# A linear-attention block on one core: two x tiles transposed on TensorE instead of three, the last head group padded to the full array, VectorE's part of each q tile placed apart in the order, and the last output tile cut finer

## The chip, the cores and the metric

The kernel runs on one core of one Trainium2 chip. Times are device microseconds of one execution; medians are over repeated runs. A profile shows one execution. Its span, from the first to the last instruction, is about 1.4 us shorter than the time of the same execution (100.7 against 102.13 us in the profiled run of before). In every profile here the granted TensorE clock is given as 1.000, so a kernel's runs are told apart by their times: a run more than 1.5% above the fastest one of the same kernel is called slow and left out of the ratios.

Three names recur. *Before* is the kernel before, *after* the changed one, and *the whole change* is after as well, where experiments are compared with it.

## The reference

```python
B, S, D = x.shape                 # 1, 2048, 640
H = 32; Dh = D // H               # 32 heads of 20
qkv = (x @ wqkv).reshape(B, S, 3, H, Dh).transpose(2, 0, 3, 1, 4)
q, k, v = qkv[0], qkv[1], qkv[2]
phi = lambda t: jnp.where(t > 0, t + 1, jnp.exp(t)) + 1e-6
pq, pk = phi(q), phi(k)
kv = jnp.einsum("bhsd,bhse->bhde", pk, v)
z = jnp.einsum("bhsd->bhd", pk)
num = jnp.einsum("bhqd,bhde->bhqe", pq, kv)
den = jnp.einsum("bhqd,bhd->bhq", pq, z)[..., None] + 1e-6
return (num / den).transpose(0, 2, 1, 3).reshape(B, S, D) @ wo
```

All inputs and the output are bf16.

## The kernel before

The work on TensorE comes in stages:

- *K*: `x·wk` per tile of 128 rows; ScalarE and VectorE turn it into `pk`.
- *P*: `xᵀ·pk`, 640x640, accumulated over the 16 row tiles in two column halves. V itself is never formed: `wvᵀ·P` gives K·V.
- *q tiles*: `x·wq`, 20 pieces of 128 columns by 512 rows, put between the other matmuls.
- *K·V groups and folds*: six groups of six heads (120 columns; the last has two heads, 40 columns). Each is masked to its block diagonal on VectorE and multiplied by its rows of `wo` ("fold").
- *den*: the denominators, in two halves ("pairs"); their inverses are spread over the partitions by DMA and multiplied into `pq` ("normalize").
- *output*: `pq·folded wo`, 16 row tiles.

A scheduler class records every operation with the names it reads and writes, and derives the semaphore waits. **Every engine's instructions are emitted in the order of recording**, so where an operation is recorded decides what it queues behind: in before, VectorE starts the mask at 68.05 us, after the add recorded ahead of it (67.71 us, once the relu is there), though the last K·V matmul had started at 67.06 us. The parts that the change touches:

```python
GW, NG = 120, 6
gsz = [min(GW, D - GW * g) for g in range(NG)]       # 120 x5, 40
...
NPE = 3          # x tiles transposed on TensorE; the others by DMA transpose
XCH = [(0, 128), (128, 256), (256, 384),
       (384, 640), (640, 1024), (1024, 1536), (1536, 2048)]
...
# loads at the start, by queue: w01 is weight chunk 0 of wk, x12 is x tile 1
for eng, what in (("sp", "w01 w23 w34 x23"), ("act", "x12 w12 w45")):
...
def q_tile(sbk, c, b, two_act=False):
    ...                                    # five matmuls of 512 columns into bank b
    P.add("act", ... activation(t, bank(b), Exp) ...)
    if two_act:
        P.add("act", ... activation(r, bank(b), Relu) ...)
    P.add("dve", ... tensor_scalar(t, t, 1.0, 1e-6, min, add) ...)
    if two_act:
        P.add("dve", ... tensor_tensor(dst, t, r, add) ...)    # waits for the relu
        return
    P.add("dve", ... scalar_tensor_tensor(dst, bank(b), 0.0, t, max, add) ...)

def kv_group(h, b):                        # K.V of three groups
    for g in range(3 * h, 3 * h + 3):
        n = gsz[g]
        m = 128 if g < 5 else n            # the last group: a 128x40 array
        for d in range(NC_):
            e.matmul(bank(b, n, off=128 * (g % 3), parts=m), wv[...+ m], pt[...+ n], ...)

def w2_half(g, h, b):                      # half a fold
    n = gsz[g]                             # the last group: a 40x40 array
    e.matmul(bank(b, HALF, parts=n), kvt[0:n, GW * g:GW * g + n], wog[0:n, ...], ...)
...
# one letter per recorded step: p P step, q/Q q tile (Q: relu on ScalarE), z/s sums of pk for the
# denominators, k/K first and second K.V group with its mask, 0 to 5 folds, n normalize, i/I den,
# T output tile
for a in "qzzppzppzzpppqpQppqppppQppzQQkzQpp2zqpQppppsppppi0pqqpppp1npnpnQKnnQn35Qnn4qnqqQQnTT
          ITnTnnTTnnnnTnTTnnTTTTTT":
    step[a]()
```

(`...` marks the cuts.)

Of the kernel before, what the change touches and what calls it, by code (L numbers as in the profile page):

```python
# [7 lines left out]
ALU = mybir.AluOpType  # L8
# [9 lines left out]
class Plan:  # L18
# [6 lines left out]
    def __init__(self, nc, es):  # L25
        self.nc, self.es = nc, es
        self.sem = {e: es(nc.semaphore(f"s_{e}")) for e in self.ENGINES}
        self.count = {e: 0 for e in self.ENGINES}
        self.ops = {e: [] for e in self.ENGINES}
        self.known = {e: {} for e in self.ENGINES}  # L30
        self.writers, self.readers = {}, {}
        self.n_dma = 0
        self.sem_obj = {f"e:{e}": s for e, s in self.sem.items()}

    def add(self, eng, fn, reads=(), writes=(), dma=False, after=()):
        op = Op()
        op.eng, op.fn, op.dma = eng, fn, dma
        deps = list(after)
        for r in reads:
            w = self.writers.get(r)  # L40
            if w is None:
                raise KeyError(f"nothing wrote {r}")
            if not (w.eng == "pe" and eng == "pe"):
                deps.append(w)
        for r in writes:
            for d in [self.writers.get(r)] + self.readers.get(r, []):
                if d is not None and (d.dma or dma or d.eng != eng):
                    deps.append(d)
        known = self.known[eng]
        waits = {}  # L50
        for d in sorted(set(deps), key=lambda o: -o.val):
            if known.get(d.sem, 0) >= d.val:
                continue
            waits[d.sem] = max(waits.get(d.sem, 0), d.val)
            for s, v in d.clock.items():
                known[s] = max(known.get(s, 0), v)
            known[d.sem] = max(known.get(d.sem, 0), d.val)
        op.waits = list(waits.items())
        if dma:
            key = f"d:{self.n_dma}"  # L60
            self.sem_obj[key] = self.es(self.nc.semaphore(f"s_dma{self.n_dma}"))
            self.n_dma += 1
            op.sem, op.val, op.inc = key, 16, 16
        else:
            self.count[eng] += 1
            op.sem, op.val, op.inc = f"e:{eng}", self.count[eng], 1
        op.clock = dict(known)
        self.ops[eng].append(op)
        for r in reads:
            self.readers.setdefault(r, []).append(op)  # L70
        for r in writes:
            self.writers[r] = op
            self.readers[r] = []
        return op
# [8 lines left out]
def bass_standalone__linear_attn_block__prompt_kernel(nc, x, wqkv, wo, out):  # L83
    B, S, D = x.shape
    assert (B, S, D) == (1, 2048, 640)
    H, DH = 32, 20
    NC_ = D // 128
    NT = S // 128
# [7 lines left out]
    with contextlib.ExitStack() as ctx:  # L96
# [50 lines left out]
        def pool_const():  # L147
            P.add("pool", lambda e: e.memset(ident[:, :], 0.0), writes=["ident"])
            P.add("pool", lambda e: e.affine_select(
                out=ident[:, :], in_=ident[:, :], pattern=[[-1, 128]], base=0,  # L150
                channel_multiplier=1, compare_op=ALU.not_equal, fill=1.0),
                reads=["ident"], writes=["ident"])
            P.add("dve", lambda e: e.memset(eps[:, :], 1e-6), writes=["eps"])
            P.add("pool", lambda e: e.memset(wv[:, NC_ * D:], 0.0), writes=["wvpad"])
            P.add("pool", lambda e: e.memset(hm[:, :], 1.0), writes=["hm"])

            def band(t, pat, base, mult, name):

                v = t.rearrange("p (a b) -> p a b", b=pat[1][1])
                P.add("pool", lambda e: e.affine_select(  # L160
                    out=v, in_=v, pattern=pat, base=base, channel_multiplier=mult,
                    compare_op=ALU.is_ge, fill=0.0), reads=[name], writes=[name])


            band(hm[:, :], [[-4, 32], [0, 1]], 0, 1, "hm")
            band(hm[:, :], [[4, 32], [0, 1]], 3, -1, "hm")

            P.add("pool", lambda e: e.memset(bm[:, :], 1.0), writes=["bm"])
            for lo in (True, False):
                band(bm[:, :], [[-DH if lo else DH, NG], [0, DH]],  # L170
                     0 if lo else DH - 1, 1 if lo else -1, "bm")


        NPE = 3
        XCH = [(0, 128), (128, 256), (256, 384),
               (384, 640), (640, 1024), (1024, 1536), (1536, 2048)]

        def xch_of(row):
            return next(i for i, (a, b) in enumerate(XCH) if a <= row < b)
# [50 lines left out]
        def load_wk():  # L230
# [4 lines left out]
            for eng, lo in (("sp", 0), ("act", HALF)):  # L235
                P.add(eng, lambda e, lo=lo: e.dma_start(
                    xn[:, lo:lo + HALF], x[0, 0:128, lo:lo + HALF]),
                    writes=[("xn", 0, lo)], dma=True)
            for eng, what in (("sp", "w01 w23 w34 x23"), ("act", "x12 w12 w45")):
                for k in what.split():  # L240
                    a, b = int(k[1]), int(k[2])
                    if k[0] == "x":
# [9 lines left out]

        def load_rest():
            w_cols(wqn, 0, D, 0, "wqn", "sp")
            for a, b in ((3, 8), (8, 12), (12, 16)):
                load_xn(a, b, "sp")
            w_cols(wv, 0, D, 2 * D, "wv", "sp")
            P.add("sp", lambda e: e.dma_start(
# [60 lines left out]
                      reads=[("bank", d)], writes=[("pt", d, h)])  # L319

        nq = [0]

        def q_tile(sbk, c, b, two_act=False):
            i = nq[0] % 4
# [14 lines left out]
            if two_act:  # L339
                r = rq[i]  # L340
                P.add("act", lambda e: e.activation(r[:, :], bank(b), ACTF.Relu),  # L341
                      reads=[("bank", b), "table"], writes=[("rq", i)])
            P.add("dve", lambda e: e.tensor_scalar(  # L343
                t[:, :], t[:, :], 1.0, 1e-6, ALU.min, ALU.add),
                reads=[("eq", i)], writes=[("eq", i)])
            dst = pq[:, c * S + BK * sbk:c * S + BK * (sbk + 1)]
            if two_act:
                P.add("dve", lambda e: e.tensor_tensor(dst, t[:, :], rq[i][:, :], ALU.add),  # L348
                      reads=[("rq", i), ("eq", i)], writes=[("pq", sbk, c)])
                return  # L350
            P.add("dve", lambda e: e.scalar_tensor_tensor(  # L351
                pq[:, c * S + BK * sbk:c * S + BK * (sbk + 1)], bank(b), 0.0, t[:, :],
                ALU.max, ALU.add),
                reads=[("bank", b), ("eq", i)], writes=[("pq", sbk, c)])

        def z_add(dst, d_ap, a, b, ra, rb):
            P.add("dve", lambda e: e.tensor_tensor(d_ap, a, b, ALU.add),  # L357
# [48 lines left out]
        def kv_group(h, b):  # L406

            def mm(e):
                for g in range(3 * h, 3 * h + 3):
                    n = gsz[g]  # L410
                    m = 128 if g < 5 else n
                    for d in range(NC_):
                        r = e.matmul(  # L413
                            bank(b, n, off=128 * (g % 3), parts=m),
# [16 lines left out]
                    writes=[("kvt", g) for g in range(lo, lo + n)])  # L431

        def w2_half(g, h, b):
            n = gsz[g]
            P.add("pe", lambda e: e.matmul(  # L435
                bank(b, HALF, parts=n), kvt[0:n, GW * g:GW * g + n],
                wog[0:n, g * D + HALF * h:g * D + HALF * (h + 1)], start=True, stop=True),
                reads=[("kvt", g), "wog", "wog5"], writes=[("bank", b)])

        def w2_group(g, b):  # L440
# [71 lines left out]
        def out_dma(st, lo, hi, eng="sp"):  # L512
            j = st % 4
            P.add(eng, lambda e: e.dma_start(
                out[0, 128 * st:128 * st + 128, lo:hi], osb[j][:, lo:hi]),
                reads=[("osb", j, c) for c in range(lo // 160, hi // 160)],
                writes=[("out", st, lo)], dma=True)
            out_keys.append(("out", st, lo))

# [1 line left out]

        def out_evac(st, b, lo, hi, eng):
            j = st % 4
            keys = [("osb", j, c) for c in range(lo // 160, hi // 160)]
            if eng == "act":
                P.add("act", lambda e: e.copy(osb[j][:, lo:hi], bank(b, hi - lo)),  # L526
                      reads=[("bank", b)], writes=keys)
# [8 lines left out]
            out_evac(st, b + 1, HALF, D, "dve")  # L536
            out_dma(st, 0, D)

        def out_last(st, b):
            q = HALF // 2  # L540
            for n, (lo, hi, eng) in enumerate(((0, HALF, "act"), (HALF, HALF + q, "act"),
                                               (HALF + q, D, "dve"))):
                out_mm(st, b[n], lo, hi)
                out_evac(st, b[n], lo, hi, eng)
            out_dma(st, 0, HALF + q)
            out_dma(st, HALF + q, D, "act")


        pool_const()
        load_wk()  # L550
# [2 lines left out]
        warm(6)  # L553
        transpose_x(0, (6, 7), ("dve", "act"))
        warm(1)
        order = "t1 k00 k10 k01 k11 k02 k12 k03 k13 t2 k04 k14"
        for k in order.split():
            st = int(k[1])
            if k[0] == "t":
                transpose_x(st, *{1: ((4, 5), ("dve", "act")), 2: ((6, 7), ("dve", "act"))}[st])  # L560
            else:
                for h in range(2):
                    k_half(st, h, (int(k[2]),))
        for st in range(2):
            k_phi(st)
        for st in range(2, NT):
            for cs in ((0, 1), (2, 3, 4)) if st < 3 else (range(NC_),):
                for h in range(2):
                    k_half(st, h, cs)
            k_phi(st)  # L570
        zst = z_steps()
        qs = [(s, c) for s in range(NSB) for c in range(NC_)]
# [71 lines left out]
        def next_out():  # L644
            st = tiles.pop(0)
            out_tile(st, pair(st))
            if st == 1:
                small[:] = [1]

        step = {"p": lambda: steps.pop(0)(),  # L650
                "q": next_q, "Q": lambda: next_q(True), "z": lambda: zst.pop(0)(),
                "n": lambda: work(1), "s": lambda: z_finish(take()),
                "i": lambda: inverse(0), "I": lambda: inverse(1),
                "k": early_kv, "0": lambda: fold_wo(0), "1": lambda: fold_wo(1),
                "2": lambda: fold_wo(2), "K": late_kv, "3": lambda: late_w2(3),
                "4": lambda: late_w2(4), "5": lambda: late_w2(5), "T": next_out}
        for a in "qzzppzppzzpppqpQppqppppQppzQQkzQpp2zqpQppppsppppi0pqqpppp1npnpnQKnnQn35Qnn4qnqqQQnTTITnTnnTTnnnnTnTTnnTTTTTT".replace(" ", ""):
            step[a]()
        assert not (qs or zst or steps or todo or tiles)
        out_last(NT - 1, (0, 1, 2))  # L660

        for name, eng in (("sp", nc.sync), ("pool", nc.gpsimd), ("act", nc.scalar),
                          ("dve", nc.vector), ("pe", nc.tensor)):
# [32 lines left out]
```

## Time and profile before

| | before |
|---|---|
| time, median of 3 runs | 101.91 us (101.66 to 102.16) |
| span of the profile | 100.7 us |
| TensorE busy | 97.9 us, 97% of the span |
| first P matmul starts | 27.89 us |
| first output matmul starts | 76.08 us |

The page of before: its span, the busy time of each engine with its share and instruction count, and the shares of the chain that ended last.

```profile
span 100.7 us, 1797 instructions
PE 97.9 (97%) x699; PEld 65.1 (65%) x699; DVE 63.8 (63%) x130; ACT 45.6 (45%) x87; POOL 4.2 (4%) x18
...
PE 95%; ACT 1%; DVE 1%; issue 0%; DVEq 0%
```

TensorE looks full. But a matmul's record lasts longer than the distance from its start to the next one's (379 ns against 216 for 512 columns), so "busy" hides idle time. I read the distance from one matmul's start to the next in the trace instead, and call it the spacing: 136 ns for 320 columns, 216 ns for 512, 53 ns for 120. (The timeline view merges neighbours; single starts come from narrow windows of it, or from the packed trace itself.) Whatever exceeds these spacings is time that a change can take away.

The chain is the other instrument. This is the chain of waits of before around the second K·V group (start in us, duration in us, what):

```profile
65.40 1.09 PE ps L329 x5
...
66.52 0.60 ACT eq L337
67.12 0.50 ACT rq L341
...
67.71 0.42 DVE pq L348
68.13 0.33 DVE kvt L429
...
68.51 0.86 PE ps L435 x4
69.36 1.21 PE ps L329 x5
70.57 0.27 PE ps L435 x2
```

But for the last VectorE copy at the very end, this is the only place where the chain goes through other engines. A q tile ends at 66.5 (L329), ScalarE takes its exp (L337) and relu (L341), VectorE adds them (L348), and only then masks K·V (L429), for which the folds (L435) wait. TensorE has work for part of that time, but not for all of it: the trace has 442 ns between the last q matmul and the first fold matmul, instead of 216.

Four folds then take 0.86 us where two take 0.27. The groups of TensorE in the window from 66.3 to 71 us show why (line, engine, operation, tiles, **array rows*columns**, moving operand, count, busy us, mean ns):

```profile
L435 PE MATMUL ps<-wog,kvt 120*120 120x320 bf16 x4 | 0.9, 311 | 0.1
L413 PE MATMUL ps<-pt,wv 128*128 128x120 bf16 x10 | 0.7, 216 | 0.0
L435 PE MATMUL ps<-wog,kvt 40*40 40x320 bf16 x2 | 0.4, 303 | 0.0
L413 PE MATMUL ps<-pt,wv 128*40 128x40 bf16 x5 | 0.3, 183 | 0.0
```

The mean durations look harmless; the spacings do not. Going into the 128x40 matmuls costs a spacing of 146 ns where 53 is usual, leaving them 113 where 25 is usual. The two 40x40 folds have 230 ns before them and 228 after them, where 135 to 140 is usual. Below, the extra time of such a step in array size is called its step cost; two of the recorded expectations call it a drain or a mode change. All are names only: the trace shows the time, not what the array does in it.

The third item is at the start, the TensorE timeline of before from 7.9 us (start, duration, instruction, count):

```profile
8.05 0.44 PE L193 MATMUL ps<-ident,xn 128*128 128x128 bf16 x5
8.33 1.93 PE L277 MATMUL ps<-wk,xT 128*128 128x320 bf16 x13
```

The five transposes of the third x tile hold TensorE from 8.05 to 8.33 us.

### The profile page before, as it was taken

Reading aid. Unit: us, or ns where it says so; the run is one execution under the profiler, and the core shown is the slowest. Engines: PE = TensorE matmul, PEld = TensorE weight load, DVE = VectorE, ACT = ScalarE, POOL = GpSimd, SP = SyncE. Lnnn points to the kernel's source line nnn. Section 1 sums busy time; section 2 is a strip of 40 time slices with the busy share of each in tenths; the row PEclk is TensorE's granted clock in tenths of the full one; section 3 lists DMA queues with packets and bytes.
Section 4 is the critical chain, followed back from the end, with each engine's and each line's share of the span. In section 5 each row is a group of like instructions: output and inputs, shape, how many; then the busy total and the mean of one; then the engine's idle time right before and its main releaser. Section 6 shows DMA issues by size and latency. Waiting matters only on the chain.

```text
span 100.7 us, 1797 instructions
## 1 busy us (share of the span) xinstructions
PE 97.9 (97%) x699; PEld 65.1 (65%) x699; DVE 63.8 (63%) x130; ACT 45.6 (45%) x87; POOL 4.2 (4%) x18
## 2 busy tenths in 40 slices
PE   6999999999999999999999999999999999999992
PEld 2557777777766665655767875864556677777771
DVE  0102998888885999438899502958697418953331
ACT  5116654445522024257674036758868523333222
POOL 6300000000000000000000420000000000000000
PEclk9999999999999999999999999999999999999999
DMA  1999989999993000000002002420220234533334
GB/s 52 298 297 229 222 138 207 372 372 363 359 213 80 0 0 0 0 3 0 3 7 61 0 0 48 114 70 0 81 61 0 93 89 121 198 134 127 130 130 130
DMA packets 17748, 12.09 MB, mean 120 GB/s; under 512 B 9293, under 2 KB 17741, under 8 KB 17741
## 3 DMA queue, kind: packets, MB, share of 16 engines
q1 hardware_dynamic: 17021, 11.38, 41.2%
q10 hardware_dynamic: 720, 0.61, 1.8%
q8 instruction: 5, 0.08, 0.4%
q14 instruction: 2, 0.02, 0.1%
HBM read 5.90 MB, written 2.62 MB: 85 GB/s over the span
## 4 chain that ended last, share of the span: by engine, by line
PE 95%; ACT 1%; DVE 1%; issue 0%; DVEq 0%
PE ps L277 22%; PE ps L504 22%; PE ps L329 20%; PE ps L304 18%; PE ps L613 4%; PE ps L267 3%; PE ps L435 2%; PE ps L193 1%; PE ps L472 1%; PE ps L413 1%; ACT eq L337 1%; ACT rq L341 0%; DVE pq L348 0%; DVE kvt L429 0%; DVE osb L529 0%; PE ps L394 0%
## 5 line engine op out<-in xcount | busy, mean ns | idle before, releaser
L329 PE MATMUL ps<-xT,wqn 128*128 128x512 bf16 x100 | 23.9, 380 | 0.0
L277 PE MATMUL ps<-wk,xT 128*128 128x320 bf16 x160 | 23.0, 307 | 0.0
L504 PE MATMUL ps<-w2p,pq 128*128 128x320 bf16 (+1 forms) x165 | 22.1, 295 | 0.0
L277 PEld LDWEIGHTS ps<-wk,xT 128*128 128x128 bf16 x160 | 15.9, 100 | 6.5 <-DMA wk<-in_wqkv_dram 0.3
L337 ACT ACTIVATE eq<-ps 128x512 bf16<-128x512 f32 x20 | 12.0, 599 | 17.8 <-PE ps L329 17.8
L504 PEld LDWEIGHTS ps<-w2p,pq 128*128 128x128 bf16 x165 | 15.8, 98 | 6.2 <-issue 0.2
L304 PE MATMUL ps<-pk,xn 128*128 128x360 bf16 (+1 forms) x130 | 19.5, 299 | 0.0
L329 PEld LDWEIGHTS ps<-xT,wqn 128*128 128x128 bf16 x100 | 11.5, 118 | 8.0 <-issue 0.3
L304 PEld LDWEIGHTS ps<-pk,xn 128*128 128x128 bf16 x130 | 12.6, 98 | 6.0
L290 ACT ACTIVATE ek<-ps 128x640 bf16<-128x640 f32 x16 | 11.2, 705 | 8.7 <-PE ps L277 8.7
L295 DVE SCALAR_TENSOR_TENSOR pk<-ps,ek 128x640 bf16<-128x640 f32 x16 | 13.2, 824 | 0.6
L343 DVE TENSOR_SCALAR eq<-eq 128x512 bf16<-128x512 bf16 x20 | 5.8, 288 | 11.7 <-ACT eq L337 11.6
L529 DVE CAST osb<-ps 128x320 bf16<-128x320 f32 (+1 forms) x16 | 7.6, 478 | 8.3 <-PE ps L504 8.3
L526 ACT CAST osb<-ps 128x320 bf16<-128x320 f32 (+1 forms) x17 | 7.0, 417 | 12.7 <-PE ps L504 11.0
L497 DVE TENSOR_TENSOR pq<-pq,rd 128x512 bf16<-128x512 bf16 x20 | 7.7, 415 | 1.9 <-DMA rd<-rdc 1.9
L292 DVE TENSOR_SCALAR ek<-ek 128x640 bf16<-128x640 bf16 x16 | 5.2, 325 | 2.8 <-ACT ek L290 2.7
L341 ACT ACTIVATE rq<-ps 128x512 bf16<-128x512 f32 x11 | 6.5, 592 | 0.0
L351 DVE SCALAR_TENSOR_TENSOR pq<-ps,eq 128x512 bf16<-128x512 f32 x9 | 6.2, 692 | 0.3
L348 DVE TENSOR_TENSOR pq<-eq,rq 128x512 bf16<-128x512 bf16 x11 | 4.7, 425 | 2.0 <-ACT rq L341 1.5
L357 DVE TENSOR_TENSOR za<-pk 128x1280 f32<-128x1280 bf16 x4 | 5.7, 1483 | 0.0
L207 DVE COPY xT<-ps 128x256 bf16<-128x256 bf16 x3 | 0.9, 291 | 6.9 <-PE ps L193 6.9
L613 PE MATMUL ps<-pk,xn 128*128 128x360 bf16 (+1 forms) x30 | 4.7, 299 | 0.0
(42 smaller groups left out, 47.8 us busy)
## 6 DMA issues: line engine op xcount, KB each, us to landing
out_dram<-osb SPq DMA_DIRECT2D x15, 160.0 KB, 1.8
xn<-in_x_dram SPq DMA_DIRECT2D x2, 640.0 KB, 8.6
wqn<-in_wqkv_dram SPq DMA_DIRECT2D x1, 800.0 KB, 5.6
xn<-in_x_dram SPq DMA_DIRECT2D x1, 800.0 KB, 7.3
wv<-in_wqkv_dram SPq DMA_DIRECT2D x1, 800.0 KB, 10.8
wog<-in_wo_dram SPq DMA_DIRECT2D x1, 750.0 KB, 12.7
w2p<-w2g SPq DMA_DIRECT2D x5, 150.0 KB
rd<-rdc SPq DMA_DIRECT2D x8, 64.0 KB, 2.2
```

The source lines that it names most:

```text
L277: r = e.matmul(bank(b + h, HALF), xT[:, c * S + 128 * st:c * S + 128 * st + 128], wk[:, c * D + HALF * h:c * D + HALF * (h + 1)], start=(c ...
L290: P.add("act", lambda e: e.activation(fold(t[:, :]), two_banks(b), ACTF.Exp), reads=banks + ["table"], writes=[("ek", st % 3)])
L295: P.add("dve", lambda e: e.scalar_tensor_tensor(fold(pk[:, st * D:(st + 1) * D]), two_banks(b), 0.0, fold(t[:, :]), ALU.max, ALU.add), rea ...
L304: r = e.matmul(bank(d, PW[h]), xn[:, st * D + 128 * d:st * D + 128 * d + 128], pk[:, st * D + PO[h]:st * D + PO[h] + PW[h]], start=(st == ...
L329: r = e.matmul(bank(b), wqn[:, d * D:(d + 1) * D].rearrange("p (q c) -> p c q", c=NC_)[:, c, :], xT[:, d * S + BK * sbk:d * S + BK * (sbk ...
L337: P.add("act", lambda e: e.activation(t[:, :], bank(b), ACTF.Exp), reads=[("bank", b), "table"], writes=[("eq", i)])
L341: P.add("act", lambda e: e.activation(r[:, :], bank(b), ACTF.Relu), reads=[("bank", b), "table"], writes=[("rq", i)])
L497: P.add("dve", lambda e: e.tensor_tensor(v, v, rd[i][:, BK * h:BK * (h + 1)], ALU.mult), reads=[("rd", i, 2 * h), ("rd", i, 2 * h + 1), (" ...
L504: r = e.matmul(bank(b, hi - lo), pq[:, c * S + 128 * st:c * S + 128 * st + 128], w2p[:, c * D + lo:c * D + hi], start=(c == 0), stop=(c == ...
L526: P.add("act", lambda e: e.copy(osb[j][:, lo:hi], bank(b, hi - lo)), reads=[("bank", b)], writes=keys)
L529: P.add("dve", lambda e: e.tensor_copy(osb[j][:, lo:hi], bank(b, hi - lo)), reads=[("bank", b)], writes=keys)
L613: r = e.matmul(bank(d, PW[h]), xn[:, st * D + 128 * d:st * D + 128 * d + 128], pk[:, st * D + PO[h]:st * D + PO[h] + PW[h]], start=False, ...
```

## The change

Its intent is to take these pieces of TensorE time away. The third x tile is transposed by DMA (DMA_TRANSPOSE in the trace; the recorded texts say "crossbar"); the last group is padded with zeros so that the array keeps its size; the VectorE part of a q tile becomes a step of its own (`d`), which can be recorded later than the q tile, so that other VectorE work need not queue behind it; and the last output tile is cut finer, so that its last copy is shorter. The core of the diff:

```diff
+            P.add("dve", lambda e: e.memset(wog[:, 5 * D:], 0.0), writes=["wog5"])
+            P.add("dve", lambda e: e.memset(kvt[:, 5 * GW:], 0.0), writes=[("kvt", 5)])
...
-        NPE = 3
-        XCH = [(0, 128), (128, 256), (256, 384),
-               (384, 640), (640, 1024), (1024, 1536), (1536, 2048)]
+        NPE = 2
+        XCH = [(0, 128), (128, 256),
+               (256, 512), (512, 896), (896, 1408), (1408, 2048)]
...
-            for eng, what in (("sp", "w01 w23 w34 x23"), ("act", "x12 w12 w45")):
+            for eng, what in (("sp", "w01 w23 w34"), ("act", "x12 w12 w45")):
...
+            held = [("eq", i), ("rq", i)] + ([] if two_act else [("bank", b)])
+            P.held.update(held)
+            def vector_part():
+                P.held.difference_update(held)
+                P.add("dve", ... min, add ...)
+                P.add("dve", ... add the relu, or max with the bank ...)
+            q_rest.append(vector_part)
...
-                    m = 128 if g < 5 else n
+                    m = 128
...
-                bank(b, HALF, parts=n), kvt[0:n, GW * g:GW * g + n],
-                wog[0:n, g * D + HALF * h:g * D + HALF * (h + 1)], start=True, stop=True),
+                bank(b, HALF, parts=GW), kvt[0:GW, GW * g:GW * (g + 1)],
+                wog[0:GW, g * D + HALF * h:g * D + HALF * (h + 1)], start=True, stop=True),
...
-        def out_last(st, b):          # 320 (act) / 160 (act) / 160 (dve)
+        def out_last(st):             # 320 (act) / 160 (dve) / 80 (act) / 80 (dve)
...
-        order = "t1 k00 k10 k01 k11 k02 k12 k03 k13 t2 k04 k14"
+        order = "t1 k00 k10 k01 k11 k02 k12 k03 k13 k04 k14"
...
-        for a in "qzzppzppzzpppqpQppqppppQppzQQkzQpp2zqpQppppsppppi0pqqpppp1npnpnQKnnQn35Qnn4qnqqQQnTTITnTnnTTnnnnTnTTnnTTTTTT"
+        for a in "QpppdpzpQqzqppppzdzpzpdqQzdpddzpqpppdQkpQzpQppdsppdpp2pp0dinQpppp1pdpQpnnpQKnndnndQ35q4qdqqdnddqddQdTTInnnTnnTnnnnTTnTTnTTnTTTTT"
```

(The two comments at `out_last` and the short forms in `vector_part` stand for longer code.) In the stretch `QKnndnndQ35` the two q tiles recorded last ahead of `K` have their `d` only after the mask, each behind two normalizes.

More of the change, by code (lines that the diff above doesn't have):

```diff
@@ L32, in __init__ @@
         self.n_dma = 0
+        self.held = set()
         self.sem_obj = {f"e:{e}": s for e, s in self.sem.items()}
@@ L38, in add @@
         deps = list(after)
+        assert not self.held.intersection(writes)
         for r in reads:
@@ L153, in pool_const @@
             P.add("dve", lambda e: e.memset(eps[:, :], 1e-6), writes=["eps"])
-            P.add("pool", lambda e: e.memset(wv[:, NC_ * D:], 0.0), writes=["wvpad"])
+            P.add("dve", lambda e: e.memset(wv[:, NC_ * D:], 0.0), writes=["wvpad"])
+            P.add("dve", lambda e: e.memset(wog[:, 5 * D:], 0.0), writes=["wog5"])
+            P.add("dve", lambda e: e.memset(kvt[:, 5 * GW:], 0.0), writes=[("kvt", 5)])
             P.add("pool", lambda e: e.memset(hm[:, :], 1.0), writes=["hm"])
@@ L254, in load_rest @@
             w_cols(wqn, 0, D, 0, "wqn", "sp")
-            for a, b in ((3, 8), (8, 12), (12, 16)):
+            for a, b in ((2, 8), (8, 12), (12, 16)):
                 load_xn(a, b, "sp")
@@ L321, in bass_standalone__linear_attn_block__prompt_kernel @@
         nq = [0]
+        q_rest = []
         def q_tile(sbk, c, b, two_act=False):
@@ L342, in q_tile @@
                       reads=[("bank", b), "table"], writes=[("rq", i)])
-            P.add("dve", lambda e: e.tensor_scalar(
-                t[:, :], t[:, :], 1.0, 1e-6, ALU.min, ALU.add),
-                reads=[("eq", i)], writes=[("eq", i)])
             dst = pq[:, c * S + BK * sbk:c * S + BK * (sbk + 1)]
-            if two_act:
-                P.add("dve", lambda e: e.tensor_tensor(dst, t[:, :], rq[i][:, :], ALU.add),
-                      reads=[("rq", i), ("eq", i)], writes=[("pq", sbk, c)])
-                return
-            P.add("dve", lambda e: e.scalar_tensor_tensor(
-                pq[:, c * S + BK * sbk:c * S + BK * (sbk + 1)], bank(b), 0.0, t[:, :],
-                ALU.max, ALU.add),
-                reads=[("bank", b), ("eq", i)], writes=[("pq", sbk, c)])
+            held = [("eq", i), ("rq", i)] + ([] if two_act else [("bank", b)])
+            P.held.update(held)
+            def vector_part():
+                P.held.difference_update(held)
+                P.add("dve", lambda e: e.tensor_scalar(
+                    t[:, :], t[:, :], 1.0, 1e-6, ALU.min, ALU.add),
+                    reads=[("eq", i)], writes=[("eq", i)])
+                if two_act:
+                    P.add("dve", lambda e: e.tensor_tensor(dst, t[:, :], rq[i][:, :], ALU.add),
+                          reads=[("rq", i), ("eq", i)], writes=[("pq", sbk, c)])
+                else:
+                    P.add("dve", lambda e: e.scalar_tensor_tensor(
+                        dst, bank(b), 0.0, t[:, :], ALU.max, ALU.add),
+                        reads=[("bank", b), ("eq", i)], writes=[("pq", sbk, c)])
+            q_rest.append(vector_part)
         def z_add(dst, d_ap, a, b, ra, rb):
@@ L433, in w2_half @@
         def w2_half(g, h, b):
-            n = gsz[g]
             P.add("pe", lambda e: e.matmul(
-                bank(b, HALF, parts=n), kvt[0:n, GW * g:GW * g + n],
-                wog[0:n, g * D + HALF * h:g * D + HALF * (h + 1)], start=True, stop=True),
+                bank(b, HALF, parts=GW), kvt[0:GW, GW * g:GW * (g + 1)],
+                wog[0:GW, g * D + HALF * h:g * D + HALF * (h + 1)], start=True, stop=True),
                 reads=[("kvt", g), "wog", "wog5"], writes=[("bank", b)])
@@ L515, in out_dma @@
                 out[0, 128 * st:128 * st + 128, lo:hi], osb[j][:, lo:hi]),
-                reads=[("osb", j, c) for c in range(lo // 160, hi // 160)],
+                reads=[("osb", j, c) for c in range(lo // 80, hi // 80)],
                 writes=[("out", st, lo)], dma=True)
@@ L523, in out_evac @@
             j = st % 4
-            keys = [("osb", j, c) for c in range(lo // 160, hi // 160)]
+            keys = [("osb", j, c) for c in range(lo // 80, hi // 80)]
             if eng == "act":
@@ L537, in out_tile @@
             out_dma(st, 0, D)
-        def out_last(st, b):
-            q = HALF // 2
-            for n, (lo, hi, eng) in enumerate(((0, HALF, "act"), (HALF, HALF + q, "act"),
-                                               (HALF + q, D, "dve"))):
-                out_mm(st, b[n], lo, hi)
-                out_evac(st, b[n], lo, hi, eng)
-            out_dma(st, 0, HALF + q)
-            out_dma(st, HALF + q, D, "act")
+        def out_last(st):
+            q = HALF + 160
+            for b, (lo, hi, eng) in enumerate(((0, HALF, "act"), (HALF, q, "dve"),
+                                               (q, q + 80, "act"), (q + 80, D, "dve"))):
+                out_mm(st, b, lo, hi)
+                out_evac(st, b, lo, hi, eng)
+            out_dma(st, 0, q)
+            out_dma(st, q, D, "act")
         pool_const()
@@ L559, in bass_standalone__linear_attn_block__prompt_kernel @@
             if k[0] == "t":
-                transpose_x(st, *{1: ((4, 5), ("dve", "act")), 2: ((6, 7), ("dve", "act"))}[st])
+                transpose_x(st, (4, 5), ("dve", "act"))
             else:
@@ L566, in bass_standalone__linear_attn_block__prompt_kernel @@
         for st in range(2, NT):
-            for cs in ((0, 1), (2, 3, 4)) if st < 3 else (range(NC_),):
-                for h in range(2):
-                    k_half(st, h, cs)
+            k_half(st, 0)
+            k_half(st, 1)
             k_phi(st)
@@ L650, in bass_standalone__linear_attn_block__prompt_kernel @@
         step = {"p": lambda: steps.pop(0)(),
-                "q": next_q, "Q": lambda: next_q(True), "z": lambda: zst.pop(0)(),
+                "d": lambda: q_rest.pop(0)(), "q": next_q, "Q": lambda: next_q(True), "z": lambda: zst.pop(0)(),
                 "n": lambda: work(1), "s": lambda: z_finish(take()),
@@ L656, in bass_standalone__linear_attn_block__prompt_kernel @@
                 "4": lambda: late_w2(4), "5": lambda: late_w2(5), "T": next_out}
-        for a in "qzzppzppzzpppqpQppqppppQppzQQkzQpp2zqpQppppsppppi0pqqpppp1npnpnQKnnQn35Qnn4qnqqQQnTTITnTnnTTnnnnTnTTnnTTTTTT".replace(" ", ""):
+        for a in "QpppdpzpQqzqppppzdzpzpdqQzdpddzpqpppdQkpQzpQppdsppdpp2pp0dinQpppp1pdpQpnnpQKnndnndQ35q4qdqqdnddqddQdTTInnnTnnTnnnnTTnTTnTTnTTTTT".replace(" ", ""):
             step[a]()
-        assert not (qs or zst or steps or todo or tiles)
-        out_last(NT - 1, (0, 1, 2))
+        assert not (q_rest or qs or zst or steps or todo or tiles)
+        out_last(NT - 1)
         for name, eng in (("sp", nc.sync), ("pool", nc.gpsimd), ("act", nc.scalar),
```

## The prediction

> **What bounds the kernel now.** TensorE: the page has it busy for 97.9 of 100.7 us, the chain of waits is 95% TensorE. A busy matmul row can hide waste, so I read the spacing of matmul starts in the timeline: 136 ns for 320 columns, 216 for 512, 53 for 120, nearly everywhere from 7 to 98 us. The excess is local:
> - the first seven K matmuls at 267 ns (slow clock): 0.9 us;
> - the third x tile's transposes: 0.28 us;
> - second K·V group, stepping from 128- to 40-column outputs: spacings 146 and 113 ns instead of 53 and 25: about 0.2 us;
> - the folds after it: 0.23 us waiting for the mask (the chain leaves TensorE only here: ScalarE exp 0.60, relu 0.50, VectorE add 0.42, mask 0.33), and about 0.25 us around the two 40-row folds (spacings 230, 150, 228, 247 against 140, 140, 140, 216).
>
> [...]
>
> **What the change does.**
> 1. Third tile by crossbar: −0.28 us, critical. Its chunk (rows 256-512) is needed at about 8.6 us. Before, the equally large first chunk was issued at 3.1 and landed at 8.4; one x load ahead of it is gone, so it should be issued at 2.65 and land at 7.9. Later chunks: about 10.5 (needed 11.3), 14 (15.4), 19 (20.8).
> 2. Padding: the last group's matmuls keep their columns (40, 320)[...]: −0.2 us (K·V), −0.25 us (folds). Three added memsets fall into VectorE's idle first 3.8 us.
> 3. VectorE part apart: the mask no longer queues behind a q tile's add that waits for ScalarE; one q tile (1.08 us) covers mask (0.40+0.18) and latencies: −0.23 us. From 28 to 65.2 us TensorE is within 1% of the sum of spacings, so reordering there gains nothing; it moves other engines' idle time.
>    Risk: a normalize of the second pair now stands before output tile 2's VectorE copy. The spread landed 3.8 us after the denominator's end, so that copy runs about 4.3 us after it instead of 1.5; its banks are needed after 5.4. Later copies keep 0.4 us, as do VectorE's copies before the first K·V group (behind 1.40 us z additions). Tight, but no stall expected.
> 4. Last tile split 320/160/80/80: same columns; the last VectorE copy shrinks from 325 to about 240 ns (estimate from 492 ns for 320 columns, 325 for 160): −0.08 us. The final store (1.5 us to landing) stays.
>
> Sum: 0.28+0.2+0.25+0.23+0.08 = about 1.05 us, nearly all critical.
>
> **Prediction: 100.9 us** (before 101.91), 80% range 100.3 to 101.5. Faster by over 2%: 0.03; within: 0.96; slower: 0.01.
>
> **What would show it.**
> - 1: five transposes fewer; K spacing 136 ns without a gap near 8.6, 11.3, 15.4, 20.8 us; outputs begin about 1 us sooner than 76.1.
> - 2: no 40x40 or 128x40 arrays; spacing near 25 ns for 40-column matmuls, 140 for folds.
> - 3: exp, relu, add and mask gone from the chain; VectorE waits for the spread before output tile 2's copy, without a TensorE gap.
> - 4: last matmul start to end of span 0.1 us shorter than 2.2.
> - Busy times nearly as before.
>
> **What would make it wrong.** A chunk landing late (TensorE gap in 8 to 21 us, up to 1 us); output tiles stalled for PSUM banks while VectorE waits for the spread; the first K·V group waiting for VectorE's copies; 40-column matmuls with full weights spaced wider than 25 ns; the slow clock at the start lasting longer.

The sum came to about 1.05 us, with the 0.2 and 0.25 us of step 2 estimated from the spacings listed at the top of the prediction.

## The result, and the profile after

The first measurement gave after a median of 100.66 us (four runs, one of them slow) and before 101.78 us. Ratios here are the mean time of one kernel's fast runs over that of the other's in the same rounds, so they are not quite the ratio of the medians quoted. This one is 0.9881 (95% interval 0.9847 to 0.9915). Three more sets of rounds of the unaltered change (again, again_b, again_c, below) gave 0.9899, 0.9925 and 0.9918. The mean of the four is 0.9906, or 0.96 us of 101.8.

The first profile of after fell into a slow run (102.74 us), so the lines of after come from the fast profile of the re-run *again*. First its page:

```profile
span 99.4 us, 1793 instructions
PE 96.2 (97%) x694; PEld 64.8 (65%) x699; DVE 64.1 (64%) x133; ACT 45.2 (45%) x86; POOL 4.5 (5%) x17
...
PE 96%; ACT 1%; issue 0%; DVE 0%
```

Five of the 699 matmul records are missing in this trace (694 against 699 weight loads); where a q tile shows "x4", its fifth matmul was run but not recorded. The chain of waits around the second K·V group:

```profile
64.80 1.08 PE ps L334 x5
65.88 0.64 PE ps L424 x15
66.53 0.07 issue
66.60 1.03 PE ps L334 x4
67.63 0.55 PE ps L445 x4
68.17 1.08 PE ps L334 x5
69.25 0.27 PE ps L445 x2
```

ScalarE and VectorE are gone from this part of the chain. K·V (L424), the next q tile and the four folds (L445) follow each other, and the four folds take 0.55 us, twice the 0.27 of two. The chain now leaves TensorE at another place, where it did not before, ahead of the q tile that follows the first half of the denominators:

```profile
57.73 0.15 PE ps L445
57.88 0.02 issue
57.91 0.76 ACT w2g L464 x2
58.67 0.18 issue
58.84 1.03 PE ps L334 x4
```

It costs nothing that the spacings show: from the last matmul of the denominators to that q tile it is 205 ns (in again_c, where no record is missing), the same as after the second half of the denominators, where the chain stays on TensorE (205 ns in before as well).

The groups in the window from 65.7 to 70 us:

```profile
L445 PE MATMUL ps<-wog,kvt 120*120 120x320 bf16 x6 | 1.1, 298 | 0.0
L424 PE MATMUL ps<-pt,wv 128*128 128x120 bf16 x10 | 0.7, 216 | 0.0
L424 PE MATMUL ps<-pt,wv 128*128 128x40 bf16 x5 | 0.3, 180 | 0.0
```

In this window no array is narrower than 120. The 40-column matmuls now run against full 128-column weights, still at 25 ns spacing. The start, in the TensorE timeline of again:

```profile
4.35 0.71 PE L197 MATMUL ps<-ident,xn 128*128 128x128 bf16 x5
4.86 4.41 PE L281 MATMUL ps<-wk,xT 128*128 128x320 bf16 x26
```

There is no third group of transposes.

To see where the time went, I cut every profile at two events that all kernels share: the start of the first P matmul and that of the first output matmul, both read from the TensorE timeline. The last column is the time from there to the end of the span.

| profile | first P at | first P to first output | first output to end |
|---|---|---|---|
| before | 27.89 | 48.18 | 24.66 |
| after, first profile (slow run) | 29.22 | 47.45 | 24.67 |
| again | 27.30 | 47.45 | 24.67 |
| again_b | 27.20 | 47.46 | 24.67 |
| again_c | 27.36 | 47.45 | 24.68 |
| transpose_only | 27.21 | 48.19 | 24.65 |
| padding_only | 28.08 | 47.96 | 24.65 |
| order_only | 27.83 | 47.90 | 24.65 |
| tail_only | 27.47 | 48.18 | 24.67 |
| after_no_padding | 27.52 | 47.90 | 24.68 |
| after_mask_queued | 27.32 | 47.94 | 24.68 |
| early_x1 | 27.49 | 47.45 | 24.66 |
| keep_busy | 27.34 | 47.46 | 24.67 |
| keep_busy_b | 27.04 | 47.45 | 24.68 |

This table is the main finding. The middle stretch repeats within 0.01 us wherever the program does the same there, on different chips and sets of rounds, and takes one of five values by what it does. The last stretch stays within 0.03 us. In these 14 profiles all other variation is in the start, and there before the 21st K matmul (the first that needs the third x tile): from its start to the first P matmul each of them takes 19.02 or 19.03 us.

### The profile page after: what moved, and what is told of

Same layout as the page of the kernel before. It is cut to its first block, busy times and chain, and to the rows that moved or that the text cites. A ratio compares the mean times of both kernels' runs of the same rounds, so it can differ in the third digit from the quotient of the medians.

```text
span 101.4 us, 1793 instructions
## 1 busy us (share of the span) xinstructions
PE 97.2 (96%) x694; PEld 65.4 (65%) x699; DVE 64.0 (63%) x133; ACT 45.2 (45%) x86; POOL 4.5 (4%) x17
## 4 chain that ended last, share of the span: by engine, by line
PE 91%; DMA 4%; ACT 1%; issue 1%; DVE 0%
PE ps L281 23%; PE ps L514 22%; PE ps L334 21%; PE ps L308 17%; DMA xn<-in_x_dram 4%; PE ps L621 4%; PE ps L445 1%; PE ps L424 1%; ACT w2g L464 1%; PE ps L197 1%; PE ps L482 1%; ACT L238 0%; DVE osb L539 0%; PE ps L405 0%
## 5 line engine op out<-in xcount | busy, mean ns | idle before, releaser
L334 PE MATMUL ps<-xT,wqn 128*128 128x512 bf16 x95 | 22.6, 379 | 0.4 <-ACT w2g L464 0.2
L514 PE MATMUL ps<-w2p,pq 128*128 128x320 bf16 (+2 forms) x170 | 22.1, 291 | 0.0
L539 DVE CAST osb<-ps 128x320 bf16<-128x320 f32 (+2 forms) x17 | 7.7, 462 | 6.3 <-PE ps L514 6.3
L413 POOL TENSOR_SCALAR zb<-hm,zc 128x32 bf16<-128x32 bf16 x5 | 2.1, 444 | 52.6 <-DVE zc L410 52.6
```

The source lines that it names most:

```text
L334: r = e.matmul(bank(b), wqn[:, d * D:(d + 1) * D].rearrange("p (q c) -> p c q", c=NC_)[:, c, :], xT[:, d * S + BK * sbk:d * S + BK * (sbk ...
L514: r = e.matmul(bank(b, hi - lo), pq[:, c * S + 128 * st:c * S + 128 * st + 128], w2p[:, c * D + lo:c * D + hi], start=(c == 0), stop=(c == ...
L539: P.add("dve", lambda e: e.tensor_copy(osb[j][:, lo:hi], bank(b, hi - lo)), reads=[("bank", b)], writes=keys)
```

## The experiments

Whole times of before spread over about 1 us (101.27 to 102.42 in one set), so effects of 0.2 to 0.5 us are read from the table above, with the whole times as a check.

### The whole change again (again, again_b, again_c)

No edit.

> The whole change once more, unaltered, since the profile of after fell into the slow state (second x tile landed at 5.4 us instead of 4.4, slow clock until 9 us instead of 6.7). Theory (four local savings on TensorE): 1.0 to 1.1 us faster than before in fast runs, the five-transpose group gone, no exp/relu/add/mask in the chain. Rival (the gain is mostly a luckier start, earlier landing or shorter slow clock): in a fast profile K would start earlier than 4.95 us, or fewer than seven K matmuls would have the 267 ns spacing, while the later stages take as long as before.

Measured: 100.78 us against 101.81, ratio 0.9899 (0.9868 to 0.993), all runs fast.

> The whole change unaltered once more, on the same chip and in the same rounds as keep_busy. Theory: 1.0 to 1.2 us faster than before in fast runs; 47.45 us from the first P matmul to the first output matmul and 24.67 us from there to the end, as in its other profiles; only the stretch before the first P matmul differs from run to run. Rival: if the middle or the last stretch varies too, the differences of 0.2 to 0.5 us between the experiments cannot be put down to their edits.

Measured: 100.88 us against 101.58, ratio 0.9925 (0.9902 to 0.9947).

> The whole change unaltered, in the same rounds as keep_busy_b, as its comparison: 1.0 to 1.1 us faster than before in fast runs, the middle and last stretches again 47.45 and 24.67 us.

Measured: 100.79 us against 101.75, ratio 0.9918 (0.9893 to 0.9944).

Two of the three ratios are a little short of the 1.0 us expected (0.76 and 0.83 us of 101.6 and 101.75). The middle stretch is 0.73 us shorter in all three, as expected, and the last one is unchanged. "Luckier start" is therefore not the main cause: 0.73 of the 0.96 us on average come from the middle. It does matter for the rest: in again K starts 0.09 us sooner than in before and has three fully slow spacings instead of seven.

### One part at a time

**transpose_only**: before, with this part alone.

```diff
-NPE = 3
+NPE = 2        # with the new chunks, no load of x tile 2, no "t2"
```

> Before with the crossbar part alone (two tiles on TensorE). Theory: 0.28 us faster than before, TensorE without a gap at 8.6, 11.3, 15.4 and 20.8 us. Rival (the gain is mostly at the start): 0.6 us or more. If a crossbar chunk lands late: a gap in 8 to 21 us and no gain.

Measured: 101.31 us against 101.81, ratio 0.9955 (0.9918 to 0.9992). The middle and last stretches are those of before. There is no gap for the DMA transposes. The gain of 0.46 us is more than 0.28, but the interval includes 0.28 us (a ratio of 0.9972). The rival's 0.6 us is not needed, though the interval reaches it too. The traces give the size more closely than the times: the spacing that holds the five transposes is 415 ns instead of 136 in each of the four profiles that have them (before, padding_only, order_only, tail_only), which is 0.28 us, and transpose_only has no such spacing. This profile had no K spacing of 267 ns: its second x tile landed late (5.02 us), and I take the clock to have risen by then, since the transposes of that tile start 57 ns apart instead of about 107 as in the other profiles (in before they are 107 ns apart ahead of the record of the full clock at 6.83 us, and 56 ns after it). Its one wide K spacing (245 ns) is a wait for VectorE's copy of the transposed tile.

**padding_only**: before, with the padding alone.

```diff
-m = 128 if g < 5 else n
+m = 128         # and w2_half on 120 rows, with the zeroed pads
```

> Before with the padding alone. Theory: the 40-column K.V matmuls at 25 ns spacing without the 146 and 113 ns steps, the folds at 140 ns; 0.4 us less on TensorE if the mask wait of 0.23 us stays as it was, so 0.35 to 0.5 us faster. Rival (the wide spacings come from the wait for the mask[...], not from array size): the spacings stay near 180 to 230 ns, at most 0.1 us faster.

Measured: 101.74 us against 101.81, ratio 0.9985 (0.994 to 1.003). The step costs are gone, as expected: K·V's 40-column matmuls are 25 ns apart, the folds 136. But the middle stretch fell by 0.22 us only, half of the step costs. Both theories failed: the spacings do come from the array size, yet the time does not fall by their sum. The chain of waits of padding_only shows where the other half went:

```profile
65.60 1.09 PE ps L331 x5
...
66.71 0.60 ACT eq L339
67.31 0.50 ACT rq L343
...
67.90 0.43 DVE pq L350
68.33 0.33 DVE kvt L431
...
68.70 0.75 PE ps L436 x4
69.45 1.08 PE ps L331 x5
```

From the end of the q tile to the folds it is the same 2.0 us as in before (66.71 to 68.70; before 66.52 to 68.51), since it runs through ScalarE and VectorE. K·V on TensorE now ends 0.2 us sooner, so TensorE waits that much longer: the spacing ahead of the folds is 656 ns, a wait of 0.44 us instead of 0.23. Only the step costs *after* the mask, around the folds, were saved.

**order_only**: before, with the placed order alone.

```diff
-"...pnpnQKnnQn35Qnn4..."
+"...pnnpQKnndnndQ35q4..."    # and d as a step of its own
```

> Before with the placed order alone (same instructions, other places). Theory: the 0.23 us wait for the mask goes, the mode-change spacings (146, 230 ns) stay; 0.2 to 0.25 us faster. Rival (the order also shortens or lengthens other stages): TensorE gaps elsewhere differ, above all in 28 to 65 us, and the time differs from before by more than 0.35 us or rises.

Measured: 101.46 us against 101.81, ratio 0.9957 (0.9921 to 0.9993). The middle stretch fell by 0.28 us. The spacing ahead of the folds is 215 ns, so the wait of 0.23 us is gone; the first fold's own spacing fell from 183 to the usual 140. The spacings with a step cost (146 and twice 228 ns) are all still there. The rest of the middle stretch is unchanged to 0.01 or 0.02 us, although most of the order is new.

**tail_only**: before, with the finer last tile alone.

```diff
-320 (act) / 160 (act) / 160 (dve)
+320 (act) / 160 (dve) / 80 (act) / 80 (dve)
```

> Before with the last tile's split alone (320/160/80/80 instead of 320/160/160). Theory of the prediction: 0.08 us off the stretch from the first output matmul to the end (24.66 us in before), by the shorter last VectorE copy. Rival, from the traces so far (24.67 us in the re-run of the whole change): nothing is gained, because ten 80-column matmuls take 36 ns each against 34.5 for half of 160 columns, VectorE comes to its last copy straight from the one before it, and the last store lands about 0.2 us after the other store, which starts no earlier. Then the stretch stays within 0.03 us of 24.66.

Measured: 101.75 us against 101.53, ratio 1.0014 (0.9988 to 1.0041). The last stretch is 24.67 us: no gain. In again the last copy did shrink from 325 to 241 ns, as these groups of VectorE in the last microseconds show, first of before:

```profile
L529 DVE CAST osb<-ps 128x160 bf16<-128x160 f32 x1 | 0.3, 325 | 0.9 <-PE ps L504 0.9
```

and of again:

```profile
L539 DVE CAST osb<-ps 128x160 bf16<-128x160 f32 x1 | 0.3, 324 | 0.5 <-PE ps L514 0.5
L539 DVE CAST osb<-ps 128x80 bf16<-128x80 f32 x1 | 0.2, 241 | 0.0
```

But the end did not follow. In before, the small store was issued 0.39 us after the large one and landed 0.22 us after it (99.15 and 98.76, landed 100.69 and 100.47). In again it was issued only 0.28 us after it, and landed 0.18 us after it (97.76 and 97.48, landed 99.39 and 99.20). The small store took 1.54 us in before and 1.63 in again. In the other profiles of the new tail the distance of the landings is 0.17 us. Counted from the first output matmul, the small store was issued 0.07 us sooner (23.00 us in tail_only, 23.07 in before) but took 0.08 us longer (1.62 us, 1.54), so the earlier issue was lost in the store itself. Ten 80-column matmuls also take 36 ns each, where half of 160 columns took 34.5. Why the store took longer is not shown; that it waits for the large one, which landed just before it, is possible, but no run separates the two.

### One part taken out of the whole change

**after_no_padding**: after, with the old array sizes.

> The whole change without the padding. Theory (padding is worth its 0.44 us of drains only where the mask is no longer late): first P matmul to first output matmul rises from 47.46 to 47.9 us, 0.45 us slower than the whole change; drains of 146 and about 230 ns come back in the K.V group and the folds, no wait for the mask. Rival (padding is worth what it gave by itself, 0.23 us): rises by 0.2 to 0.25 us only.

Measured: 101.25 us against 101.53, ratio 0.9967 (0.994 to 0.9995). The middle stretch rose from 47.45 to 47.90 us: 0.45, and the rival's 0.2 to 0.25 is out. The spacing ahead of the folds is 216 ns, so there is no wait; the step costs are back (spacings of 146 and 112 ns in K·V, 227 and 228 around the folds). Padding is thus worth 0.45 us with the placed order and 0.22 without it.

**after_mask_queued**: after, with two letters of the order moved, nothing else.

```diff
-"...QpnnpQKnndnndQ35q4..."
+"...QpnnpQddKnnnnQ35q4..."   # the pending VectorE parts ahead of the mask
```

> The whole change, but the VectorE parts of the two pending q tiles put back ahead of the second K.V mask, as in before. Nothing else moves. Theory (the mask is late because VectorE waits in order for the last q tile's relu on ScalarE): a TensorE gap of about 0.44 us returns before the folds, as with padding alone, and the time is 0.4 to 0.45 us over the whole change. Rival (the order helped through something else, for instance ScalarE's or bank waits elsewhere): no gap there, within 0.1 us of the whole change.

Measured: 101.32 us against 101.53. One of its six runs, 102.54 us, was above all others and still counted as fast, so its ratio (0.9998, 0.9956 to 1.004) is of little use. The middle stretch is 47.94 us, 0.49 more than the whole change. Its chain of waits:

```profile
64.81 1.09 PE ps L334 x5
...
65.93 0.60 ACT eq L342
66.53 0.50 ACT rq L346
...
67.46 0.41 DVE kvt L440
...
67.92 0.75 PE ps L445 x4
```

The detour over exp, relu and mask is back by moving two letters. The spacing ahead of the folds is 653 ns, a wait of 0.44 us, and the first fold takes 183 ns again instead of 140. So the mask's place in VectorE's queue is what the order gained, and the rest of the new order is neutral for TensorE.

### The start

The first profile of after is slow by its start alone (first P at 29.22 us; the rest of its table row is that of the fast ones). Its TensorE timeline:

```profile
3.87 0.63 PE L271 MATMUL ps<-const-bfloat16-1.0 128*128 128x512 bf16 x1
5.47 0.71 PE L197 MATMUL ps<-ident,xn 128*128 128x128 bf16 x5 [0.97 <-DMA xn<-in_x_dram]
```

The second x tile landed at 5.43 us instead of 4.3 to 5.0 in the fast profiles with the same loads, and TensorE sat idle. Then twelve K spacings instead of seven were wide (eleven of 267 ns, about twice the usual 136, and one of 204; the page of this profile has no row of granted clock), until 9.0 us. I take them for the slow clock, since before has the same 267 ns until 6.83 us, where its trace records the full clock as granted, and 136 from then on. In the fast profiles the spacings became normal at 6.9 us or sooner, in keep_busy_b before 5.25 us and in transpose_only before 5.1 us. The packed traces of seven profiles also hold the moment at which the full clock was granted, and it agrees with the spacings: 6.83 us in before, 5.37 in again_b, 5.51 in again_c, 5.23 in keep_busy_b. The slow profile has no such record. What sets the moment is not shown. Idle time alone does not decide it: in early_x1 (below) TensorE sat idle for 1.03 us until 5.75 us, about as long as in the slow profile, and yet the full clock was granted at 5.36 us. What makes a run slow stays open.

**early_x1**: after, with x tile 1 loaded in halves by both queues ahead of the weights, and a shorter filler.

```diff
-sp: x0a w01 w23 w34      act: x0b x12 w12 w45
+sp: x0a x1a w01 w23      act: x0b x1b w12 w34 w45
-warm(1)
+warm(1, 128)
```

> The whole change, with the second x tile loaded in halves by both queues ahead of all weights, and the filler matmul between the two transposed tiles cut from 512 to 128 columns. Theory (the start is set by when the second x tile lands, 4.3 to 5.4 us over six profiles): it lands near 3.8 us, the first weights near 4.5; K starts near 4.5 instead of 4.9 to 5.4; 0.2 to 0.5 us faster than the whole change, if the crossbar chunk does not land later than about 8.3 us. Rival (the start is set by the weights' bandwidth and by when the clock rises): K waits for its second or third weight chunk or for the crossbar chunk, and nothing is gained.

Measured: 101.31 us against 101.53, ratio 0.9963 (0.9937 to 0.9989), and two of its six runs were slow (103.0 and 103.26 us); before, too, had one slow run of 11 in these rounds (103.1 us). The tile landed at 3.67 us, as expected, but the first weight chunk at 5.70 instead of the expected 4.5, as the TensorE timeline shows:

```profile
5.75 4.52 PE L279 MATMUL ps<-wk,xT 128*128 128x320 bf16 x32 [1.03 <-DMA wk<-in_wqkv_dram]
```

The rival was right that K waits for a weight chunk (the bandwidth and the clock's rise that it gave as causes were not tested): whatever each queue issued third, at 1.70 us, landed at 5.3 to 6.1 us in every profile. Putting x first put the weights third.

**keep_busy** and **keep_busy_b**: after, with two filler matmuls between the transposed tiles.

```diff
-warm(1)
+warm(2)
```

> The whole change with two 512-column filler matmuls between the two transposed tiles instead of one, so that TensorE is busy until about 4.73 us even if the second x tile lands late. Theory[...]: K starts at 5.2 to 5.3 us instead of 4.9, a delay of 0.4 us of which about half is lost because the clock is still slow then, so 0.1 to 0.3 us slower than the whole change among fast runs, but no run as slow as 102.5 us. Rival (the slow runs come from the transfers alone): slow runs stay as frequent as with one filler.

("About half" is an estimate from the two K spacings, 267 and 136 ns.)

Measured: 100.64 us against 101.58, ratio 0.9899 (0.9875 to 0.9923), where again_b in the same rounds had 0.9925. It was expected to be slower and was not. K did start late (5.25 us), but in again_b and in keep_busy K waits for its second weight chunk, which landed at 5.95 and 6.09 us, so an earlier start gains nothing. None of the six runs of either was slow, so nothing was learnt about slow runs.

> The kernel of keep_busy again, on another set of rounds. Theory, formed from its first profile (a later K start costs nothing, since K then waits for its second weight chunk, which lands near 5.9 us, and the longer filler only fills time that TensorE would have spent waiting): 0.0 to 0.3 us faster than the unaltered change in the same rounds. Rival (the 0.24 us of the first rounds were luck of the start): within 0.1 us, or slower.

Measured: 100.66 us against 101.75, ratio 0.9906 (0.9883 to 0.993); again_c in the same rounds 0.9918. Both times keep_busy was the faster, by 0.24 and 0.13 us in the medians, but the intervals overlap. It beats before clearly; that it beats after is not settled.

**The DMA-transposed chunk.** The profiles of the whole change also show that step 1 is tighter than predicted. This is what TensorE's weight loads waited for in again_c (who, for what: us in total, times, longest):

```profile
PEld ps L281 <- DMA xT<-in_x_dram: 0.4, 1, 0.4
PEld ps L281 <- DMA wk<-in_wqkv_dram: 0.3, 1, 0.3
```

The first DMA-transposed chunk landed at 8.28 us there, and the K matmul spacing at 7.91 us is 415 ns instead of 136: 0.28 us lost, just what leaving the transposes out had saved. In again it landed at 8.23 and cost 0.09 us; in again_b at 8.00 and cost nothing.

## Why the prediction was right or wrong

The predicted 100.9 us (its terms add up to a gain of 1.05) met 100.66 us at first and 100.78 to 100.88 later, a gain of 0.96 on average. The three larger mechanisms were right. That the sum came so close is in part luck, since errors in the terms cancel: the order brought 0.28 us instead of 0.23, the last tile nothing instead of 0.08, and step 1 less than 0.28 in two of three profiles.

1. *Third tile by DMA transpose, −0.28 us.* The five transposes are gone, as predicted. The mis-sized term is the slack of 0.7 us: the chunk was to land at 7.9 us and to be needed at 8.6. It landed at 7.76 to 8.34 in the kernels with this part, and where the clock rose early it was needed at about 8.0 to 8.2 us. Of the 0.28 us, 0 (again_b), 0.09 (again) and 0.28 us (again_c) were given back. The "TensorE gap in 8 to 21 us" named as a risk came true at its first place only; no later chunk was late.
2. *Padding, −0.2 and −0.25 us.* Right in the whole change: 0.45 us by after_no_padding. The prediction did not say that the first half depends on step 3. Alone, the K·V part only lengthens the wait for the mask (padding_only).
3. *VectorE part apart, −0.23 us.* Right: order_only 0.28 us, of which 0.23 are the wait and 0.04 the first fold's spacing. That it is the mask's place in the queue, and nothing else in the new order, is shown by after_mask_queued. That between 28 and 65.2 us "reordering there gains nothing" held.
4. *The risk in step 3.* VectorE does wait in order for the spread ahead of output tile 2's copy: in again 3.4 us idle, and the copy starts 4.3 us after the denominator's end, as predicted. TensorE shows no gap, and the last stretch is unchanged. The first K·V group did not wait either.
5. *Last tile, −0.08 us.* Wrong. The copy shrank as predicted (241 ns), and the small store was issued 0.07 us sooner, but the end did not move (tail_only, 24.67 against 24.66 us). The failed step is "The final store (1.5 us to landing) stays": it took 1.62 us instead of 1.54.

The middle stretch adds up: 0.28 (order) + 0.45 (padding on top of it) = 0.73 us, which is 48.18 − 47.45. (Single spacings of before and again_c, taken at the same places, differ by 0.71 us.) The rest of the 0.96 us, about 0.2, belongs to the start. It is a remainder, not a measurement: step 1's 0.28 us less what the late chunk gives back would about fill it, but first P varies by 0.3 us among kernels with the same start (27.20 to 27.52 in the fast profiles of the change and of its two variants), and the full clock and the x tile come at different times there too (5.37 and 5.51 us in again_b and again_c; 4.3 to 5.0 us).

## What to carry to other kernels

On an engine that never looks idle, list the spacings of instruction starts and explain every one that exceeds its form's usual value; here four such places (the transposes, the two steps in array size, the wait for the mask) held nearly the whole gain. The prediction's list was not complete: the two groups of matmuls for the denominators use 128x32 arrays, and the spacing is 229 ns going into the second of them, where 136 is usual, and 205 coming out, where the steps between its sets of four matmuls are about 100. Both are in before and in after, and no run tried to remove them. Here a saving ahead of a wait that another engine set (0.2 us of K·V's step costs) was worth nothing until that wait was gone (padding: 0.22 us alone, 0.45 with the placed order), so measure parts both alone and taken out of the whole, and expect the two numbers to differ. Where whole times scatter by more than the effect, cut the trace at events that all variants share: stretches that repeat within 0.01 us settle what the medians can't.

## What else the profiles measured

- Steps in array size (before): 93 ns extra entering a 128x40 array (146 against 53) and 88 leaving it (113 against 25), about 90 on either side of a 40x40 array (230 and 228 against 135 to 140). Two 120x120 folds between 128x128 matmuls (at 70.41 us) cost nothing extra (spacings of 140 and 135 ns against 136).
- Streams of weight loads and matmuls (before): 53 ns for 120 columns, 136 for 320 and 216 for 512; 25 ns for 40 columns.
- The wide K spacings at the start cost 0 to 0.9 us in fast profiles and 1.5 us in the slow one (twelve spacings, 131 ns extra each for most), up to 1.5% of the time and larger than the whole change.
- Loads issued one after another at the start: the 80 KB pieces issued at 0.8 us landed at 2.9 to 3.2, the 160 KB ones issued at 1.2 us at 4.0 to 5.4, those at 1.7 us at 5.3 to 6.1 us (in before 3.0 and 3.2, 4.1 and 4.4, 5.7 and 5.9 us); a 256-row DMA-transposed chunk issued at 2.65 us landed at 7.8 to 8.3 us (8.32 in the first profile of after).
